# Start of a recurrence: whole first loads, key decay in one piece, another order on TensorE, three tiles for the rows of a batch

## The chip, the cores and the metric

The kernel runs on one core of a Trainium2 chip. Its engines each work through a list of their own and wait for each other with semaphores: TensorE (PE, matrix products; PEld is its loading of weights), VectorE (DVE), ScalarE (ACT), GpSimd (POOL) and SyncE (SP, which here only issues transfers). Products land in PSUM, in banks of 512 numbers a partition (the tiles of lines 63 to 67); all other tiles are in SBUF. The metric is the device time of one execution in microseconds; lower is better.

## What is computed

First a linear recurrence (RWKV-5) over 4 batches, 8 heads, 768 steps, with 48 numbers per head; then a routed layer (top 1 of 8 experts, 384 to 1024 to 384) on the 3072 rows that come out:

```python
for t in range(S):
    kt, vt, rt = (k[:, :, t], v[:, :, t], r[:, :, t])
    cur = np.einsum('bhd,bhe->bhde', u[None] * kt, vt)
    y[:, :, t] = np.einsum('bhd,bhde->bhe', rt, state + cur)
    state = w[None, :, :, None] * state + np.einsum('bhd,bhe->bhde', kt, vt)
...
logits = x @ w_gate
expert_idx = np.argmax(logits, axis=1)
...
    h = np.maximum(xe @ w1[e], 0.0)
    ye = h @ w2[e]
    out[mask] = gate_w[mask, None] * ye
```

All is done in 32-bit floats. `w` (the decay, between 0.85 and 0.95 here) and `u` belong to a head and are the same for all batches.

## The kernel before, in words

The recurrence is cut into 16 *units*, each a batch and a pair of heads (4 pairs), and each unit into 6 chunks of 128 steps. Within a chunk the work is a masked product; between chunks a small state is carried. A unit goes through these steps, each a function named in the code:

- `load_rk`, `load_vk`: SP issues the transfers of r and k (channels on partitions, the two heads at partitions 0 to 47 and 64 to 111) and of v and k (steps on partitions). There are three tiles `rks` and four tiles `vks`, used in turn. The arrays in memory hold zeros in the padding rows 48 to 63.
- `scale` (VectorE): r and k times the powers of w within a chunk, into `RKs`. The powers `TT` come from `decays` (a ladder on VectorE, with squares of w from POOL).
- `pairs` (POOL, for unit 0 VectorE): r times k into `rps`. `p_own` (TensorE): its sum with u over the channels, into the bank `dsb`. `own_t` (VectorE) transposes that, and `diag` (ACT, 12 instructions) puts it on the diagonals of `Aw`.
- `p_scores` (TensorE): the products within chunks, into the banks X0, X1 and X23; `mask` (VectorE, three instructions a unit) puts their upper triangles into `Aw`.
- `keys` (POOL or VectorE): k times the decay to the end of its chunk, into `Kds`. The decay `T3` comes from `key_decay` (VectorE and a wrapped copy on POOL) and `p_key_decay` (two transposes on TensorE for each head pair, then a copy on ACT).
- `p_ds` (TensorE): what each chunk adds to the state, into `dsb`; `scan` (VectorE) runs the state over the chunks.
- `p_out` (TensorE): the output, from `Aw` and the states, into the banks `yps`; `out_t` (ACT) copies it; `p_tr` (TensorE) turns it to rows and makes the logits; `keep` (ACT) copies that into the tile `xbs` of the batch, of which there are two. `send` (POOL) sends a batch's rows to their experts' places in memory, some turns after the batch is done.

The order on each engine is that in which the code lists the instructions: nothing reorders them. After a start written out by hand (lines 728 to 762), a loop of turns (763 to 828) runs unit i together with the output of unit i - 1 and the rows of unit i - 2. A copy of one number to `turn` on POOL (lines 751, 775, 781, 835) makes POOL wait there for another engine's result. `p_fill` issues products of the identity that nothing reads. From line 832 on come the experts; that part is the same in both kernels but for one name.

Before the first turn, `p_own` and `p_out` need banks without old contents in the rows that they don't write: line 730 copies zeros there on ACT. Lines 107 and 108 clear the padding rows of `rks[1]` and `rks[2]` on VectorE, since `load_rk` brings only the 48 channels of each head for all units but the first, whose load is whole and in two halves.

`key_decay` and `p_key_decay` are called for head pair 0 first (lines 736 and 741) and for the other three later (750 and 758). `load_rk(i + 3)` stands at the head of turn i (line 766).

## Time and profile before

| | us |
|---|---|
| median of five runs | 369.79 |
| lowest and highest of the five | 369.02, 369.98 |
| the profiled execution | 368.42 |
| its span, first to last instruction | 366.2 |
| TensorE busy | 349.6 |
| VectorE, POOL, ACT busy | 265.3, 210.9, 144.9 |
| mean clock granted to TensorE | 0.983 |
| turn 1 begins (first product of `p_own(1)`) | 19.93 |
| turns 2 and 3 begin | 24.83 and 30.67 |
| the last unit's turn ends, experts begin | 112.88 |

The profiled execution is one execution, and its times are not the median's: all times within the span are its own. In the views, a row of the timeline has a start in us, a duration, the engine, the line, the operation, and what it writes and reads; neighbouring instructions of the same kind are merged with their number (x16), and brackets give idle time of the engine before it and what ended it. One `nc.tensor.matmul` of 32-bit floats shows as two matmul records, so a `p_fill(8)` is x16. The clock is a share of full speed.

### The profile page before, as it was taken

To read this page: it belongs to the slowest core of one execution; us is meant where nothing else is said; L and a number is where in the kernel's file an instruction comes from. 1 tells how busy PE (TensorE), PEld (TensorE's weight loads), DVE (VectorE), ACT (ScalarE), POOL (GpSimd) and SP (SyncE) were. 2 spreads that over 40 slices of the span, in tenths; PEclk is the share of its full clock that TensorE was granted. 3 is DMA by queue.
4 is the path that set the end of the run, shared out by engine and by line. 5 is a ranking of instruction groups with operands and counts; after the bars stand their busy time and mean duration, and the time that the engine had idled before them with its cause. 6 is when DMAs were issued, how large, how long until landed. Compare 5 with 4: busy or idle time off the path is not lost.

```text
span 366.2 us, 9907 instructions
## 1 busy us (share of the span) xinstructions
PE 349.6 (95%) x3733; PEld 331.3 (90%) x3733; DVE 265.3 (72%) x659; ACT 144.9 (40%) x416; POOL 210.9 (58%) x262
## 2 busy tenths in 40 slices
PE   5799999999999999999999999999999999999991
PEld 5588887877888999999999999999999999999891
DVE  7777887887873328693897995898688788865531
ACT  4568877877885410322323312221230321113210
POOL 4859898999975530562116407904922951999342
PEclk9599999999999999999999999999999999999998
DMA  7998998978746895978459327624742943313401
GB/s 157 260 221 221 255 235 212 247 229 210 254 115 220 266 367 99 212 222 267 123 180 218 106 56 216 177 88 139 196 151 92 204 145 130 108 52 86 147 18 52
DMA packets 35610, 63.67 MB, mean 174 GB/s; under 512 B 18922, under 2 KB 20410, under 8 KB 35553
## 3 DMA queue, kind: packets, MB, share of 16 engines
q1 hardware_dynamic: 30048, 48.39, 50.3%
q0 software_dynamic: 3776, 9.84, 7.6%
q10 hardware_dynamic: 1728, 4.72, 3.8%
q8 instruction: 31, 0.51, 0.6%
q14 instruction: 27, 0.21, 0.2%
HBM read 51.82 MB, written 11.40 MB: 173 GB/s over the span
## 4 chain that ended last, share of the span: by engine, by line
PE 79%; ACT 6%; DVE 5%; issue 4%; POOL 3%; POOLq 0%; DVEq 0%; ACTq 0%
PE X L525 12%; PE X L587 10%; PE yps L629 9%; PE X L503 8%; PE tr L629 8%; PE yps L525 5%; ACT A L331 5%; PE dsb L629 4%; PE tr L525 3%; PE dsb L525 3%; PE yps L364 3%; PE yps L587 2%; PE X L325 2%; PE tr L382 2%; PE yps L369 2%
## 5 line engine op out<-in xcount | busy, mean ns | idle before, releaser
L702 POOL DMA_INDIRECT out_dram<-yo,ix x28 | 28.4, 1014 | 68.1 <-DVE so L647 43.1
L331 ACT ACTIVATE A<-eyes,own 128x128 f32<-128x128 f32 x192 | 58.0, 391 | 11.6 <-DVE own L315 10.1
L337 DVE COPY_PREDICATED A<-strict,X 128x512 f32<-128x512 int32 x48 | 34.7, 737 | 9.2 <-ACT xb L388 4.6
L587 PE MATMUL X<-hT,w2s 128*128 128x160 f32 (+5 forms) x288 | 36.5, 287 | 0.0
L587 PEld LDWEIGHTS X<-hT,w2s 128*128 128x128 f32 x288 | 36.2, 191 | 0.2
L436 POOL DMA_INDIRECT rows<-xb,slot x24 | 28.1, 1171 | 12.6 <-issue 5.1
L629 PE MATMUL yps<-tums,sums 128*128 128x192 f32 x184 | 32.3, 326 | 0.0
L629 PEld LDWEIGHTS yps<-tums,sums 128*128 128x128 f32 x184 | 30.3, 190 | 0.0
L702 POOL DMA_INDIRECT out_dram<-yt,it x16 | 16.8, 1048 | 20.5 <-DVE yt L654 9.4
L289 DVE TENSOR_TENSOR RK<-rk,TT 112x1536 f32<-112x1536 f32 (+1 forms) x17 | 27.7, 1636 | 0.0
L295 POOL TENSOR_TENSOR rp<-rk 112x768 f32<-112x768 f32 x15 | 27.3, 1817 | 0.0
L525 PE MATMUL X<-xT,w1s 128*128 128x208 f32 (+5 forms) x120 | 26.0, 331 | 0.0
L325 PEld LDWEIGHTS X<-RK 48*64 48x64 f32 x768 | 18.8, 137 | 7.6 <-issue 5.1
L716 POOL TENSOR_TENSOR tums<-w2s,tums 128x384 f32<-128x384 f32 x24 | 24.7, 1029 | 0.4
L364 PE MATMUL yps<-A,vk 128*48 128x128 f32 x384 | 24.0, 274 | 0.0
L325 PE MATMUL X<-RK 48*64 48x128 f32 (+1 forms) x768 | 21.9, 254 | 2.1 <-DVE RK L289 2.1
L525 PEld LDWEIGHTS X<-xT,w1s 128*128 128x128 f32 x120 | 20.9, 190 | 0.0
L364 PEld LDWEIGHTS yps<-A,vk 128*48 128x48 f32 x384 | 20.2, 123 | 0.4
L658 ACT ACTIVATE so<-so,xg 128x192 f32<-128x192 f32 x24 | 10.0, 450 | 25.2 <-DVE so L647 25.2
L663 ACT COPY so<-tr 128x192 f32<-128x192 f32 x7 | 2.2, 318 | 44.4 <-PE tr L629 44.4
L629 PE MATMUL tr<-w2s,hT 128*128 128x192 f32 x112 | 19.4, 326 | 0.0
L554 ACT ACTIVATE hT<-hT 128x416 f32<-128x416 f32 (+5 forms) x23 | 12.3, 537 | 17.6 <-DVE hT L546 17.6
(220 smaller groups left out, 842.9 us busy)
## 6 DMA issues: line engine op xcount, KB each, us to landing
w1s<-in_w_dram SPq DMA_DIRECT2D x36, 384.0 KB, 3.2
w2s<-in_w_dram SPq DMA_DIRECT2D x24, 384.0 KB, 3.4
rk<-in_rk_dram SPq DMA_DIRECT2D x30, 288.0 KB, 6.0
vk<-in_vk_dram SPq DMA_DIRECT2D x16, 528.0 KB, 5.5
w2s<-in_w_dram ACTq DMA_DIRECT2D x8, 384.0 KB, 5.9
xs<-rows SPq DMA_DIRECT2D x16, 169.0 KB, 5.6
w1s<-in_w_dram ACTq DMA_DIRECT2D x4, 384.0 KB, 3.3
rows<-zt SPq DMA_DIRECT2D x4, 312.0 KB, 4.8
```

Of the source, the lines that this page charges most:

```text
L289: nc.vector.tensor_tensor(RKs[i % 3][0:KP].rearrange("p u (c t) -> p u c t", t=C)[:, :, c0:c1], x[0:KP].rearrange("p u (c t) -> p u c t", ...
L295: (eng or nc.gpsimd).tensor_tensor(rps[i % 2][0:KP], x[0:KP, 0], x[0:KP, 1], op=ALU.mult)
L325: nc.tensor.matmul(o, lhsT=r[q, 1, c * C + 64 * z:c * C + 64 * z + 64], rhs=r[q, 0, c * C + 64 * z:(c + 1) * C], start=True, stop=True, sk ...
L331: nc.scalar.activation(A[:, place(c, h), :], eyes[:, c & 1, :], func=ACT.Copy, scale=own[i % 2][:, c, h:h + 1])
L337: nc.vector.copy_predicated(o, m, X01[k].rearrange("p (z c) t -> p z (c t)", z=2) if k < 2 else X23[:, :, 0:2 * C])
L364: nc.tensor.matmul(o(c, h), lhsT=v[:, c, h * D:(h + 1) * D], rhs=A[:, place(c, h), :], start=c < 2, stop=c == 0, skip_group_check=True)
L436: s_ = nc.gpsimd.indirect_dma_start(out=rows[:, :], out_offset=bass.IndirectOffsetOnAxis(ap=slot[b % 2][:, c:c + 1], axis=0), in_=xbs[b % ...
L503: nc.tensor.matmul(p[:, 0:self.n], lhsT=w1s[self.k % 2][f // 2][:, m, f % 2 * 128:(f % 2 + 1) * 128], rhs=self.t[:, m, 0:self.n], start=m ...
L525: nc.tensor.matmul(p[:, at * n:(at + 1) * n], lhsT=a, rhs=b, start=j == 0, stop=j == len(ab) - 1, skip_group_check=True)
L587: nc.tensor.matmul(p[:, 0:n], lhsT=w2s[self.k % 2][f // 2][:, f % 2, m * 128:(m + 1) * 128], rhs=self.h[:, f, self.c:self.n], start=f == 0 ...
L629: nc.tensor.matmul(p[:, at * Z:(at + 1) * Z], lhsT=a(f), rhs=b(f), start=f == 0, stop=f == FT // 2 - 1, skip_group_check=True)
L702: s_ = nc.gpsimd.indirect_dma_start(out=to[:, :], out_offset=bass.IndirectOffsetOnAxis(ap=at, axis=0), in_=x, in_offset=None, bounds_check ...
```

## The change

1. `xbs` has three tiles in place of two.
2. `load_rk` brings units 1 and 2 whole, padding included, in one transfer each (unit 0 whole in two halves as before, the others without padding in two transfers as before). The memsets of the padding go.
3. Zeros in the banks yps and dsb are written by VectorE's memset, at its very start, in place of ACT's copies; the tile `zero` goes.
4. `key_decay` is called once for all four head pairs. The transposes of pair 2 go to the first half and those of pair 3 to the second half of bank yps1 (before: yps0 and yps1).
5. The start on TensorE after `p_own(0)`: transposes of pair 0, the rest of `p_scores(0)`, transposes of pairs 1 to 3, `p_fill(6)`, `p_ds(0)`, `p_fill(3)`, `p_own(1)`. Before: transposes of pair 0, a third of `p_scores(0)`, `p_ds(0)`, the last third, transposes of pairs 1 to 3, `p_fill(8)`, `p_own(1)`.
6. On VectorE: `own_t(0)`, `scale(1)`, `keys(0)`, then two masks, `scan(0)` and the third mask. Before: the rest of `key_decay` behind `keys(0)`, then `scan(0)` and three masks. On POOL the order stays, with one wrapped copy in place of two.
7. `load_rk(i + 4)` stands in the middle of turn i, behind `pairs(i + 1)`, in place of `load_rk(i + 3)` at its head; unit 4 stays at the head of turn 1. On SP the transfers of r and k thus come before that turn's `load_vk(i + 3)` and not behind it.

```diff
+    for y in yps:
+        nc.vector.memset(y, 0.0)
+    nc.vector.memset(dsb, 0.0)
...
     def load_rk(i):
         if i < U:
             b, hp = divmod(i, HP)
-            if not i:
-
-                for q in (slice(0, S // 2), slice(S // 2, S)):
-                    nc.sync.dma_start(rks[0][0:KP, :, q], rk[b, hp].rearrange("h p u s -> (h p) u s")[0:KP, :, q])
-            else:
-
-                for h in range(2):
-                    nc.sync.dma_start(rks[i % 3][64 * h:64 * h + D], rk[b, hp, h, 0:D])
+
+            for q in (slice(0, S // 2), slice(S // 2, S)) if not i else (slice(0, S),) if i < 3 else ():
+                nc.sync.dma_start(rks[i % 3][0:KP, :, q], rk[b, hp].rearrange("h p u s -> (h p) u s")[0:KP, :, q])
+
+            for h in range(2) if i > 2 else ():
+                nc.sync.dma_start(rks[i % 3][64 * h:64 * h + D], rk[b, hp, h, 0:D])
...
-    for i in range(1, 3):
-        nc.vector.memset(rks[i][32:64], 0.0)
...
-    zero = cp.tile([128, 1], FP32, name="zero")
-    nc.gpsimd.memset(zero, 0.0)
...
-            o = (tr[:, 0:256], tr[:, 256:512], yps[0][:, 0:256], yps[1][:, 0:256])[hp]
+            o = (tr[:, 0:256], tr[:, 256:512], yps[1][:, 0:256], yps[1][:, 256:512])[hp]
...
-    xbs = [ca.tile([128, G, HP, Q], FP32, name=f"xb{i}") for i in range(2)]
+    xbs = [ca.tile([128, G, HP, Q], FP32, name=f"xb{i}") for i in range(3)]
...
     selection()
-    for y in (dsb, *yps):
-        nc.scalar.copy(y, bc(zero, [128, 512]))
     decays(0, HP)
     scale(0, 0, G // 2)
     p_scores(0, range(2))
     scale(0, G // 2, G)
     pairs(0, nc.vector)
-    key_decay(0, 1)
+    key_decay(0, HP)
     state_decay()
     p_own(0)
     own_t(0)
-    scale(1)
     p_key_decay(0, 1)
     p_scores(0, range(2, 4))
...
+    diag(0)
+    p_scores(0, range(4, G))
+    p_key_decay(1, HP - 1)
+    load_rk(3)
+    scale(1)
     keys(0, nc.vector)
-    diag(0)
-    load_rk(3)
-    key_decay(1, HP - 1)
+    p_fill(6, yps[0][:, 384:512])
     nc.gpsimd.tensor_copy(turn, RKs[1][0:1, 0, 0:1])
     pairs(1)
+    keys(1)
     p_ds(0)
-    scan(0)
     mask(0, 0)
     mask(0, 1)
-    p_scores(0, range(4, G))
-    p_key_decay(1, HP - 1)
-    keys(1)
+    scan(0)
     mask(0, 2)
-    p_fill(8, yps[0][:, 384:512])
+    p_fill(3, yps[0][:, 384:512])
     load_vk(3)
     for i in range(1, U):
         b, k = divmod(i - 6, 4)
         rt = i >= 6 and k == 0 and b < B - 1
-        load_rk(i + 3)
+        if i == 1:
+            load_rk(4)
         p_own(i)
...
             pairs(i + 1)
+            load_rk(i + 4)
             keys(i + 1, nc.vector if i in (7, 8, 11, 12) else None)
```

Every `xbs[b % 2]` becomes `xbs[b % 3]`.

## The prediction

> **What bounds the kernel now.** I read the page first, then who waited for whom, then the timeline of the first 40 us and the same stretch cut into windows for the clock.

> ```profile
> PE 349.6 (95%) x3733; PEld 331.3 (90%) x3733; DVE 265.3 (72%) x659; ACT 144.9 (40%) x416; POOL 210.9 (58%) x262
> ...
> PEclk9599999999999999999999999999999999999998
> ```

> TensorE is busy nearly everywhere; only the second slice (9.2 to 18.3 us) is at half clock. The waits of TensorE over the whole span:

> ```profile
> PE X L325 <- DVE RK L289: 2.1, 1, 2.1
> PE dsb L311 <- POOL rp L295: 1.8, 3, 0.9
> PE X L121 <- POOL zero L116: 1.4, 1, 1.4
> PE dsb L311 <- issue: 1.2, 1, 1.2
> PE dsb L344 <- DVE Kd L300: 1.2, 1, 1.2
> PE dsb L311 <- DVE S L349: 0.5, 1, 0.5
> ```

> Of these all but the second are before 25 us, and none is on a transfer. From turn 2 on (24.83) a turn takes 5.84 us of TensorE, save where batches are sent off. So what the change does to the time is how far it moves the first products of turn 2, p_own(2). The timeline up to there:

> ```profile
> 2.81 1.34 DVE L108 MEMSET rk<- 32x1536 f32 x1 [0.27 <-issue]
> ...
> 4.18 0.17 DVE L148 TENSOR_SCALAR pw<-wug 112x4 f32<-112x4 f32 x1
> ...
> 4.43 2.11 POOL L167 TENSOR_TENSOR pw<-pw 112x4 f32<-112x4 f32 x7 [0.93 <-DVE pw L148]
> ...
> 10.13 0.82 PE L311 MATMUL dsb<-rp,wug 112*2 112x192 f32 x8 [1.22 <-issue]
> ...
> 11.77 3.61 ACT L331 ACTIVATE A<-eyes,own 128x128 f32<-128x128 f32 x12
> ...
> 16.93 3.07 PE L121 MATMUL yps<-ident 128*128 128x128 f32 x16
> ...
> 19.93 0.51 PE L311 MATMUL dsb<-rp,wug 112*2 112x192 f32 x8
> ...
> 20.51 0.38 DVE L315 STREAM_TRANSPOSE own<-dsb 128x192 f32<-128x192 f32 x1 [3.18 <-PE dsb L311]
> ...
> 24.83 0.51 PE L311 MATMUL dsb<-rp,wug 112*2 112x192 f32 x8 [0.50 <-DVE S L349]
> ```

> Two chains are to be seen. Early, VectorE's two memsets (1.20 to 4.15) hold back the powers of w, and with them everything up to the diagonals at 11.77. Later TensorE itself is the chain: it works from 13.53 to 24.3 with no gap over 0.1, eight filler products (16.93 to 20.0) stand right before p_own(1), and rp(1), which p_own(1) reads, had been ready since 17.15. From p_own(1) on, own_t(1), the diagonals, mask and scan(1) lead 4.9 us later to p_own(2). The windows give the clock (columns: stretch, its length, PE, PEld, DVE, ACT, POOL busy, clock, DMA share, GB/s):

> ```profile
> 8.60:8.90 0.30, 0.30 (x16) 0.17 (x8) 0.30 (x1) 0.00 (x0) 0.00 (x0) 0.92 1.20 161
> 8.90:12.30 3.40, 2.18 (x28) 1.16 (x26) 2.54 (x5) 0.74 (x3) 1.94 (x3) 0.50 1.04 243
> 12.30:15.70 3.40, 2.24 (x41) 1.93 (x38) 3.40 (x6) 3.09 (x11) 3.23 (x13) 0.50 0.97 188
> 15.70:19.00 3.30, 3.21 (x15) 2.86 (x15) 1.63 (x3) 0.95 (x3) 2.75 (x3) 0.50 1.08 326
> 19.00:19.20 0.20, 0.20 (x4) 0.20 (x3) 0.00 (x0) 0.00 (x0) 0.00 (x0) 0.78 1.43 246
> ```

> The clock falls at 8.85 and is back at 19.09, 10.24 us later. A stretch of 3.4 us that is 64 or 66% busy did not bring it back; one 97% busy did. A filler pass takes 0.24 us before that edge and 0.13 after.

> **The change, part by part.** First the early chain, where the gain is. The two memsets of r and k go (2 x 1.34), three memsets of 128x512 in PSUM come. No row shows one: a third of the 1536-wide memset is 0.45, ACT's copy into the same banks 0.58, VectorE's mask of 128x512 out of PSUM 0.74. So they end between 2.55 and 3.42; I take 0.55 each, the nearest being the same engine's memset and the same bank's write: 2.85. The weights wug are there by 3.13 (ACT reads them then). But the powers run on POOL, and POOL is busy with strict and eyes until 3.50, less about 0.05 for the dropped memset of zero. The powers can start at 3.45 instead of 4.43: 0.98 gained, 0.86 at the dear end. ACT's three copies of zero (1.7 us) go too; ACT was idle behind them till 11.56, so that is worth nothing.

> Key decay whole: one product of 512 columns for one of 128 (0.28). The other 112x512 product took 0.69, so 0.41 more on VectorE, inside the 0.85 us in which it waited for p_own(0). POOL's wrapped copy grows from 64 to 256 columns (0.24 and, for 192, 0.34): 0.40, and the second transpose of head pair 0 waits for it: 0.1 lost. The later 1.18 and 0.34 go. So p_own(0) comes at 9.15, the diagonals at 10.9 instead of 11.77, and end at 14.5 instead of 15.38: 0.87 earlier.

> Now TensorE's new order. After p_own(0) and the first transposes (to 10.6) come the other two thirds of scores(0) (0.92 each, to 12.4) and the transposes of head pairs 1 and 2 (0.63 and 0.47, to 13.5). Pairs 2 and 3 now share the bank yps1, and by the built order pair 3's transposes wait for ACT's copy of pair 2. That copy stands behind the twelve diagonals and the copy of pair 1: 14.5 plus two steps of 0.35 with their end, 15.1. **Here is a new wait** of 1.6 us on TensorE, and queued behind it are six fillers, p_ds(0), three fillers and p_own(1). At half clock: transposes 0.47 to 15.57; 12 passes at 0.24, 2.84, to 18.4; p_ds(0) 1.15, of which 0.7 is done by 19.09 and the rest takes 0.26 at the ratio of its rows (0.65 against 1.15): 19.35. Then six passes at 0.13 to 20.13, beside which scan(0) (0.65, starting 0.12 after p_ds) ends at 20.12. p_own(1), which waits for scan(0), starts at 20.2: **0.3 later than 19.93**. The 0.97 gained upstream is eaten: the fillers start 1.3 earlier, but one more of them (0.47) and p_ds(0) (1.15) now stand in the row. mask(0,2) runs from 20.1 to 20.8 and own_t(1), due 20.8, just fits behind it. From there the chain of 4.3 us to p_own(2) is unchanged.

> The edits with no price, each with its cover. Whole loads of units 1 and 2: 688,128 instead of 589,824 bytes, but one issue instead of two and no wait for a memset. scale(1) would like rk at 10.4. Bytes moved by 9.0 us before: 1.41 MB, as much as wug, unit 0 and the larger unit 1 need. If it is late, scale(1) may slip 5 us before the masks (needed by scan(0) at 19.4) or scores(1) at 20.6 feel it. scale(1) and keys(0) stay behind own_t(0) on VectorE. pairs(1) on POOL: dec's copy ran until VectorE's products ended and 0.68 more; now to about 13.5, pairs(1) to 15.8, keys(1) to 17.1, both before 20.2. Loads of r and k in mid-turn: SP now issues rk(i+4) after pairs(i+1) and only then vk(i+3). In turn 1 vk(4) goes out at about 25.8 instead of 23.55, is there 5.5 later (median landing of vk) at 31.3, and is read at 35.05. The tightest is vk(12): 73.37 becomes about 74.5, lands by 80, read at 83.50; only a landing of 9 us would cost. Since no wait of TensorE is on a load, nothing can be gained. Three tiles xb: ACT's copies L387 in turns 10 and 14 (79.86, 105.34) start without idle time behind the diagonals, so the wait for the sends that goes was hidden: zero. The waits of turns 7 to 12 (rp late on POOL behind sends and sums) keep their places.

> Sum: +0.3 on the profiled execution's 368.42, so 368.7. The median of the five runs is 369.79, 1.37 above the profiled one; carried over: **370.1**.

> [...] In the new order the stretch from 8.9 to 12.3 is some 92% busy, between the 66% that did not bring the clock back and the 97% that did. If it does, the clock is full from 12.3, and then comes the stall of about 2 us at 13 to 15.1. The row: before, TensorE idled 2.07 us (6.28 to 8.35) and the clock fell at 8.85; so it would fall again at 15.7, and p_own(1) comes at 19.9: no change. [...]

> **Rivals.** *The clock is kept* (faster): granted before 13.4 and not lost in the stall. The 5.86 us of half-clock work from 15.1 (0.45 + 2.84 + 1.15 + 1.42) then takes 0.55 of that, 3.2, and p_own(1) starts at 18.35: 1.6 gained, 368.2. For it: the 92% stretch. Against: the fall at 8.85 after as short a stall. *The clock comes late* (slower): the new stall at 13.5 to 15.1 makes a 3.4 us stretch with part of it as poor as the 64% ones, so the edge may fall behind p_own(1). All 5.86 at half clock: 20.95, and p_own(1) itself 0.82 instead of 0.51: 1.3 lost, 371.1. It decides from an edge at about 20.3, where p_own(1) passes 20.67. For it: before, work ran on from 13.53, now only from 15.1. *A load is late*: vk(12) or the whole rk(1) as above; a landing of 13.5, the longest of vk, would cost vk(12)'s reader 4.5: 374. Against: that landing was in the crowded start.

> **How the numbers follow.** Edge near where it was, +0.0 to +0.3: 0.42. Clock kept, or early enough to gain over 0.74: 0.24. Clock late: 0.31; late load 0.03. 0.2% is 0.74 us, about what a measurement of this kernel can tell from none. Faster 0.24, same 0.42, slower 0.34. The likeliest alone lies in 369.6 to 370.6; with both clock cases, whose ends are 368.2 to 371.2, 8 in 10 are within 368.4 to 371.2.

> **What would show it.** Powers of w on POOL at 3.45; diagonals at 10.9; an idle TensorE from about 13.5 to 15.1, released by ACT; fillers at 15.6; p_own(1) near 20.2 and p_own(2) near 25.1, then turns of 5.84. Wrong if TensorE does not idle there, if the clock is full at 15.6, or if p_own in turns 7, 8, 9, 11 and 12 waits otherwise than by 0.26, 0.87, 0.25, 0.20 and 0.70.

## The result, and the profile after

The changed kernel takes 373.06 us in the median (369.30 to 381.59, 39 executions), the kernel before beside it 369.83 (368.58 to 374.48, 65 executions); the ratio is 1.0044, with an interval of 1.0028 to 1.0059. The ratio leaves out slow executions, those over 1.5% above the fastest of the same kernel, and the medians do not. The spread itself changed: of all executions in this study, 22 of 59 of the changed kernel were more than 5 us over the kernel before's median on the same chip, 7 of 24 of its version without the moved loads, 0 of 24 of the moved loads alone, and 3 of 181 of the kernel before. The forecast was 370.1 (368.4 to 371.2), no change likeliest; by the ratio the kernel is some 1.6 us slower, by the medians 3.2.

The first profiled execution took 376.77 us (span 374.6), so it is one of these 22. The page's busy time and clock, then the timeline of the start:

```profile
PE 353.1 (94%) x3735; PEld 334.2 (89%) x3735; DVE 267.4 (71%) x659; ACT 143.4 (38%) x413; POOL 208.3 (56%) x260
...
PEclk9599999988999999999999999999999999999997
```

```profile
3.44 2.15 POOL L164 TENSOR_TENSOR pw<-pw 112x4 f32<-112x4 f32 x7
...
9.13 0.82 PE L308 MATMUL dsb<-rp,wug 112*2 112x192 f32 x8 [1.17 <-DVE rp L292]
...
10.89 3.61 ACT L328 ACTIVATE A<-eyes,own 128x128 f32<-128x128 f32 x12
...
14.97 0.63 PE L182 MATMUL yps<-ident,T3c 112*128 112x112 f32 x2 [1.91 <-ACT T L183]
...
15.40 2.79 PE L118 MATMUL yps<-ident 128*128 128x128 f32 x12
...
18.12 1.04 PE L341 MATMUL dsb<-vk,Kd 128*48 128x48 f32 x20
...
20.08 0.51 PE L308 MATMUL dsb<-rp,wug 112*2 112x192 f32 x8
...
24.77 0.49 PE L361 MATMUL yps<-A,vk 128*48 128x128 f32 x5 [1.35 <-issue]
...
26.02 0.51 PE L308 MATMUL dsb<-rp,wug 112*2 112x192 f32 x8
```

Up to 20.08 this is the start as forecast: powers at 3.44, diagonals at 10.89, the new wait of TensorE on ACT's copy (1.91), p_own(1) at 20.08 where the kernel before has 19.93. Then comes a row that nothing in the kernel before resembles: TensorE stands still for 1.35 us in the middle of p_out(0), between two products that need nothing new, and what ended the stall is "issue": no semaphore. p_own(2) comes at 26.02 (24.83 before). Further on, in turn 10, the same happens at the transposes p_tr(8). The releaser that the row names, a diagonal on ACT, has nothing to do with these products, and yT, which they read, had been there since 77.9:

```profile
80.60 2.04 PE L379 MATMUL tr<-sel,yT 112*128 112x104 f32 x8 [1.80 <-ACT A L328]
```

The clock's windows around it (stretch, length, busy time of PE, PEld, DVE, ACT, POOL, then granted clock, DMA share, GB/s):

```profile
77.20:80.60 3.40, 1.61 (x57) 1.14 (x56) 3.23 (x9) 2.57 (x9) 3.10 (x4) 1.00 1.02 302
80.60:84.00 3.40, 3.40 (x26) 3.21 (x28) 1.32 (x2) 2.50 (x8) 3.24 (x4) 0.50 0.99 252
84.00:87.40 3.40, 3.40 (x43) 2.95 (x39) 2.15 (x7) 0.33 (x1) 0.74 (x4) 0.50 0.57 152
87.40:90.80 3.40, 3.40 (x73) 2.81 (x72) 1.88 (x2) 2.26 (x7) 2.45 (x2) 1.00 0.63 191
```

In the stretch with the stall TensorE is busy for 1.61 of 3.40 us; the next two run at half clock, and turn 10 takes 11.13 us instead of 6.51. So this execution lost 1.35 and 4.6 us in the turns of two stalls without a wait, one of them with a drop of the clock behind it. Two smaller losses in it are plain waits: p_own(8) on POOL's rp(8), behind a send that sat idle for 2.38 us for a load, and p_own(13) (1.57).

```profile
61.56 1.18 POOL L433 DMA_INDIRECT rows<-xb,slot  x1 [2.38 <-DMA rk<-in_rk_dram]
...
64.74 0.51 PE L308 MATMUL dsb<-rp,wug 112*2 112x192 f32 x8 [2.33 <-POOL rp L292]
```

**What "issue" may be.** The page's list of DMA queues has a line of 31 packets and 0.51 MB of kind "instruction", so some 16,400 bytes each (16,384 in the packets). I counted TensorE's records (a product and its weight load each, twice for 32-bit data, and the few of its sequencer) from 0 at the start of the trace. The stalls of 1.35, 0.28 (at 53.34) and 1.80 us stand before records 449, 1729 and 2753. Each of these is 193 more than a multiple of 256, as it would be if a packet held 256 of these records, 64 bytes for each; all 7557 make 29.5 such packets. *Theory F*: TensorE had run out of instructions, since the next block had not landed. Against it *theory W*: a wait on data or on another engine that the profile does not name. And on which edit costs: *theory B*, the moved loads; *theory S*, the reordered start; *theory I*, only both together.

### The profile page after: what moved, and what is told of

The parts are those of the page before. It is cut to its first block, busy times and chain, and to the rows that moved or that the text cites. A ratio compares the mean times of both kernels' runs of the same rounds, so it can differ in the third digit from the quotient of the medians.

```text
span 374.6 us, 9895 instructions
## 1 busy us (share of the span) xinstructions
PE 353.1 (94%) x3735; PEld 334.2 (89%) x3735; DVE 267.4 (71%) x659; ACT 143.4 (38%) x413; POOL 208.3 (56%) x260
## 4 chain that ended last, share of the span: by engine, by line
PE 79%; ACT 5%; issue 4%; DVE 4%; DMA 3%; POOL 3%; POOLq 0%; DVEq 0%; ACTq 0%; SPq 0%
PE X L522 12%; PE X L584 9%; PE yps L626 8%; PE X L500 8%; PE tr L626 8%; PE yps L522 5%; ACT A L328 4%; PE dsb L626 3%; PE yps L361 3%; DMA rows<-zt 3%; PE tr L522 3%; PE dsb L522 3%; PE tr L379 2%; PE yps L584 2%; PE X L322 2%
## 5 line engine op out<-in xcount | busy, mean ns | idle before, releaser
L433 POOL DMA_INDIRECT rows<-xb,slot x24 | 28.9, 1205 | 16.3 <-issue 5.4
L286 DVE TENSOR_TENSOR RK<-rk,TT 112x1536 f32<-112x1536 f32 (+1 forms) x17 | 29.7, 1754 | 1.1 <-DMA rk<-in_rk_dram 1.1
L699 POOL DMA_INDIRECT out_dram<-yt,it x16 | 16.8, 1047 | 20.5 <-DVE yt L651 9.4
L361 PE MATMUL yps<-A,vk 128*48 128x128 f32 x384 | 25.5, 283 | 1.3 <-issue 1.3
L713 POOL TENSOR_TENSOR tums<-w2s,tums 128x384 f32<-128x384 f32 x24 | 24.7, 1030 | 0.4
L361 PEld LDWEIGHTS yps<-A,vk 128*48 128x48 f32 x384 | 21.3, 128 | 2.0 <-issue 1.6
L379 PE MATMUL tr<-sel,yT 112*128 112x104 f32 x128 | 19.4, 295 | 1.9 <-ACT A L328 1.8
L655 ACT ACTIVATE so<-so,xg 128x192 f32<-128x192 f32 x24 | 10.1, 450 | 25.4 <-DVE so L644 25.4
L379 PEld LDWEIGHTS tr<-sel,yT 112*128 112x128 f32 x128 | 16.6, 199 | 3.3 <-ACT A L328 1.9
L626 PE MATMUL tr<-w2s,hT 128*128 128x192 f32 x112 | 19.4, 326 | 0.0
## 6 DMA issues: line engine op xcount, KB each, us to landing
vk<-in_vk_dram SPq DMA_DIRECT2D x16, 528.0 KB, 10.5
```

What stands on the lines that cost most here:

```text
L286: nc.vector.tensor_tensor(RKs[i % 3][0:KP].rearrange("p u (c t) -> p u c t", t=C)[:, :, c0:c1], x[0:KP].rearrange("p u (c t) -> p u c t", ...
L361: nc.tensor.matmul(o(c, h), lhsT=v[:, c, h * D:(h + 1) * D], rhs=A[:, place(c, h), :], start=c < 2, stop=c == 0, skip_group_check=True)
L379: nc.tensor.matmul(trv[c // 4][:, c % 4, :], lhsT=yTs[i % 3][0:KP, c & 1, (c // 2) * C:(c // 2 + 1) * C], rhs=sel[:, c & 1, i % HP, :], st ...
L433: s_ = nc.gpsimd.indirect_dma_start(out=rows[:, :], out_offset=bass.IndirectOffsetOnAxis(ap=slot[b % 2][:, c:c + 1], axis=0), in_=xbs[b % ...
L626: nc.tensor.matmul(p[:, at * Z:(at + 1) * Z], lhsT=a(f), rhs=b(f), start=f == 0, stop=f == FT // 2 - 1, skip_group_check=True)
L699: s_ = nc.gpsimd.indirect_dma_start(out=to[:, :], out_offset=bass.IndirectOffsetOnAxis(ap=at, axis=0), in_=x, in_offset=None, bounds_check ...
```

## Experiments

### Each part alone

On one chip: the kernel before with edit 7 alone, the changed kernel without edit 7, and the kernel before with edit 1 alone.

```diff
 # loads_mid: kernel before
-        load_rk(i + 3)
+        if i == 1:
+            load_rk(4)
...
             pairs(i + 1)
+            load_rk(i + 4)
 # loads_old: changed kernel, the same lines the other way round
 # tiles3: kernel before
-    xbs = [... for i in range(2)]
+    xbs = [... for i in range(3)]
```

> This is the kernel before with one part of the change alone: the loads of r and k for turn i+4 are issued behind the pairs of turn i+1 (and the fourth unit's at the head of turn 1), where they were issued for turn i+3 at the head of turn i. The start, the two batch tiles and the memsets stay. Theory B (the moved loads): on SyncE's queue the loads of r and k now stand ahead of the load of v and k and of the batch's clear of the rows, three in one burst, so v and k land later (median about 8 to 10.5 us from issue where the kernel before has 5.5), the clears later still (about 11 us against 4.8), and in turns 7 to 12 the first send of a batch or the keys wait for them: slower by 1 to 3 us (370.8 to 372.8 where the kernel before gives 369.8), with waits of 1 us and more before the own products of turn 8 or in the block of turn 10. Theory P (the prediction: a load that comes earlier or later within its slack gains and costs nothing): the time of the kernel before within 0.2% (369.1 to 370.5). Theory S (the reordered start costs everything): also the time of the kernel before.

> This is the changed kernel with the loads of r and k put back to the head of the turn (for turn i+3); the three batch tiles and the whole reordered start stay. Theory B (the moved loads cost most of the loss): turns 7 to 12 have the waits of the kernel before again, and what stays is the start: own products of turn 1 at about 20.1 and of turn 2 at about 25 to 26 (the 1.35 us that TensorE stands still inside the first output products in the changed kernel may stay, since it may come from the order of TensorE's instructions): 369.9 to 371.3 where the kernel before gives 369.8. Theory S (the reordered start costs everything, because it moves TensorE's program against something that runs by its own clock): as the changed kernel, 371.5 to 373, with the long turns 7, 10 and 12 still there.

> This is the kernel before with three tiles in place of two for the rows of a batch, and nothing else. The prediction priced this at nothing: no row of the kernel before shows a wait of ScalarE's copy into the tile or of GpSimd's numbers on the sends of the batch before. Expected: the time of the kernel before within 0.2%, whatever the theory on the rest. A loss or a gain of over 0.2% would say that the place of the tiles, or the numbers' earlier write, has a price that the trace of before does not show.

| | median, us | ratio to the kernel before (interval) | turns 1 and 2 begin |
|---|---|---|---|
| kernel before, same chip | 369.69 | | |
| moved loads alone | 369.79 | 1.0004 (0.9981 to 1.0027) | 20.64, 25.87 |
| all but the moved loads | 370.29 | 1.0014 (0.9989 to 1.0039) | 20.17, 25.07 |
| three tiles alone | 369.53 | 0.9988 (0.9966 to 1.0010) | 20.14, 25.05 |

Theory B expected 1 to 3 us from the moved loads and falls: by themselves they show no cost, with v and k landing 6.3 us after issue (5.5 in the kernel before; 10.5 in the first profile of the whole). Theory S expected the long turns 7, 10 and 12 without them; they were not there (7.30, 6.52 and 6.65 us in its one profile), so it falls too in this form. But 2 of the 12 executions without the moved loads took 378 us, so the start is not free in all of them. Three tiles are worth nothing, as forecast. What is left is that the parts together do what neither does, or that the first profile's chip was at fault. The edits of the start (2 to 6) were not tried one by one.

### Moving the block boundaries

Two kernels put more records on TensorE ahead of the suspected places.

```diff
 # fetch_shift: changed kernel, each of the twelve fillers at the very start as two of 64 columns (48 records more)
     for k in range(12):
-        p_fill(1, X01[k // 4][:, k % 4, :] if k < 8 else ...)
+        o = X01[k // 4][:, k % 4, :] if k < 8 else ...
+        for z in range(2):
+            nc.tensor.matmul(o[:, 64 * z:64 * z + 64], lhsT=ident, rhs=ident[:, 64 * z:64 * z + 64], ...)
 # tiny_shift: changed kernel, ahead of pair 3's transposes, where TensorE waits anyway (40 records more)
+            if hp == 3:
+                for _ in range(10):
+                    nc.tensor.matmul(yps[0][0:2, 384:392], lhsT=ident[:, 0:2], rhs=ident[:, 0:8], ...)
```

> This is the changed kernel with each of the twelve filler products at the very start split into two of 64 columns each: the same columns in sum, but 48 more instruction records on TensorE ahead of everything else. Theory F: the places where TensorE of the changed kernel stands still with no wait of its own (1.35 us inside the first output products, 1.80 us at the transposes of turn 7) are block boundaries of its instructions, all three found at places that are 193 more than a multiple of 256 instructions, where the next 16,384 bytes of instructions had not landed. Then these stalls leave the places where they were: the one of the first output products goes, because the boundary is now crossed at about 12 us instead of 16.7, so the own products of turn 2 start at about 24.9 instead of 26.0, and any stall left stands again at 193 more than a multiple of 256, some dozen products earlier in the program. Time: 0.8 to 4 us below the changed kernel's of the same chip. Theory W (the stalls are waits on data or on another engine): the stalls stay at the same products of the first output block and of turn 7's transposes, and the time is the changed kernel's within 0.3%.

> This is the changed kernel with ten products of 2 rows and 8 columns each put ahead of pair 3's transposes, where TensorE stands idle from 13.06 to 14.97 us anyway: 40 more instruction records on TensorE and, unlike the halved fillers, no time (about 1 us inside the idle). Theory F (instructions that land late): the boundary of instructions that is crossed at 16.7 in the changed kernel is crossed at about 13.3, its next block lands by 21, and the 1.35 us stall inside the first output products is gone: own products of turn 2 at 24.7 to 25.0 after those of turn 1 at 20.1; stalls left stand at places that are 193 more than a multiple of 256. Time 0.5 to 3 us below the changed kernel's. Theory B (the moved loads alone, through late v and k and late clears): turns 7 to 12 as long as in the changed kernel, time within 0.3% of it.

Both times theory F was right on the places; on the time it was wrong once and undecided once. With the halved fillers: 372.61 us, 1.0084 (1.0049 to 1.0118), in a set of runs without the changed kernel. They were not free: twice as many weight loads took 10.31 us instead of 4.67, p_own(0) came at 12.72 instead of 9.13, and that is the loss. But turn 1 took 4.91 us with no stall in it. The stalls were now before records 1473, 1729, 2497 and 2753, all again 193 more than a multiple of 256, but at other products. With the tiny products (0.65 us, inside the idle stretch), 377.73 us, 1.0016 (0.9982 to 1.0049) on a slower chip where the kernel before took 376.69. That is below the 1.0034 of the changed kernel there, as expected, but by less than the intervals can tell. In its profiled execution (383.36 us) turn 1 took 4.92, and a stall came one block later, before record 705. That is now a state product of unit 2, no longer an output product:

```profile
28.58 0.56 PE L345 MATMUL dsb<-vk,Kd 128*48 128x48 f32 x14
32.09 0.48 PE L345 MATMUL dsb<-vk,Kd 128*48 128x48 f32 x6 [2.95 <-issue]
32.30 2.84 PE L365 MATMUL yps<-A,vk 128*48 128x128 f32 x24
```

In the middle of one run of equal products, with all operands there, TensorE waits 2.95 us. Theory W falls: the stall stays at the count and not at the product. Over all profiles of this study, every stall of TensorE between 20 and 60 us that is longer than 0.25 us and has no wait of its own stands before such a record. In the packets of kind instruction, the block in question had landed shortly before each time:

| kernel | record | stall, us | block landed | TensorE went on |
|---|---|---|---|---|
| changed, first profile | 449 | 1.35 | 23.16 | 24.77 |
| changed, first profile | 2753 | 1.80 | 79.29 | 80.60 |
| halved fillers | 1729 | 1.35 | 54.52 | 56.32 |
| tiny products | 705 | 2.95 | 30.64 | 32.09 |
| first try (below) | 449 | 3.35 | 22.79 | 24.41 |
| third try (below) | 705 | 2.91 | 28.31 | 29.88 |

In the 27 such stalls of over 0.15 us, between 20 and 84 us, TensorE went on 1.20 to 1.80 us after the landing. Over the whole of all 17 profiles it enters 476 blocks, and not one sooner than 1.20 us after its landing. That is what theory F needs and what chance would not give. Most entries cost nothing of the kind: between 20 and 84 us it enters 171 blocks, and 144 of them without such a stall.

### The whole and its parts side by side

The changed kernel was run twice more, on two chips, and on the second of them together with both parts and one profile of the kernel before.

> This is the changed kernel itself once more, on the chip of the next two. Each part of the change alone left the time where it was (moved loads 1.0004 of the kernel before, the rest 1.0014), while the whole came to 1.0044 with a profiled execution of 376.8 us. Theory I (the two parts together lose what neither loses alone): median again 371 to 374, executions spread over 8 us and more, landings of v and k near 10 us, and in most profiles a stall of TensorE of over 1 us without a wait of its own. Theory C (the chip of the first measurement was to blame, whose packets took some 10% longer): median 370 to 371, landings of v and k at 5 to 7 us, no turn over 7.5 us.

> The changed kernel beside its parts on one chip. Theory I (the parts together lose what neither loses alone, because the reordered start brings TensorE to its second block boundary 1.8 us later, with less time to spare, while the moved loads keep more outstanding and so let blocks of instructions start later): 1.003 to 1.006 of the kernel before, above both parts by 0.002 and more; the parts at 0.999 to 1.0025. Theory A (the losses just add): the whole equals the sum of the two parts within 0.002. Theory C (it was chips): the whole at 0.999 to 1.002 here.

> The moved loads alone once more, beside the whole: 0.999 to 1.0025 of the kernel before by theory I; half of the whole's loss or more by theory A, if it is the loads that cost.

> The whole change without the moved loads, beside the whole: 1.000 to 1.0025 of the kernel before by theory I; half of the whole's loss or more by theory A, if it is the start that costs.

> The kernel before once more, for its profile on this chip: own products of turn 1 at 19.9 to 20.2, of turn 2 at 24.8 to 25.2, blocks of instructions that start 0 to 4 us after their crossings, and no stall of over 0.5 us without a wait before 60 us. If stalls of 1 us and more stand in it too, then late blocks alone do not set the changed kernel apart on this chip.

| | ratio to the kernel before (interval) | kernel before, median |
|---|---|---|
| whole, chip of the tiny products (again) | 1.0034 (1.0000 to 1.0068) | 376.69 |
| whole, another chip (again2) | 1.0100 (1.0035 to 1.0166) | 376.92 |
| moved loads alone, that chip | 0.9990 (0.9953 to 1.0027) | 376.92 |
| all but the moved loads, that chip | 1.0015 (0.9972 to 1.0058) | 376.92 |

Theory C (the chip) falls: the whole is slower in all three measurements, though the second interval reaches 1. Theory A (losses just add) would have 1.0005 for the whole on the last chip; the whole's interval excludes that, but the sum of the parts is itself known to only some 0.006, and the whole's six executions gave more than the 1.003 to 1.006 that theory I expected. The medians there are 381.71 us for the whole, 380.05 for all but the moved loads and 376.61 for the moved loads: in its long executions the start loses by itself. So that only the two together cost is not shown. What the stalls do is clearer from the profiles. First TensorE's waits from 5 to 60 us in the changed kernel (the last of its three profiles), then in the kernel before on the same chip (line and operand, releaser, sum, number, longest):

```profile
PE yps L182 <- ACT T L183: 2.7, 1, 2.7
PE yps L361 <- issue: 2.1, 4, 0.7
PE X L322 <- DVE RK L286: 1.5, 1, 1.5
PE dsb L308 <- DVE rp L292: 1.2, 1, 1.2
PE dsb L308 <- POOL Kd L297: 0.3, 1, 0.3
```

```profile
PE dsb L344 <- DVE Kd L300: 1.8, 1, 1.8
PE X L325 <- DVE RK L289: 1.4, 1, 1.4
PE dsb L311 <- issue: 1.2, 1, 1.2
PE dsb L311 <- DVE S L349: 0.5, 1, 0.5
PE dsb L311 <- POOL Kd L300: 0.3, 1, 0.3
```

The line with four waits for "issue" in the output products is the whole's alone; the moved loads alone and the rest alone have no such line on this chip. (The whole's second profile has three such stalls, 0.54, 0.54 and 0.96, before records 449, 705 and 961; all but the moved loads had two on its first chip, 0.18 and 0.50, and the moved loads alone one, 0.36 before record 2753.) Added up from 20 to 84 us, the stalls are 3.4, 2.0 and 2.1 us in the whole's three profiles, 0.7 and 0 without the moved loads, 0.4 and 0 with them alone, and 0 in the two of the kernel before and the one with three tiles. That is of the size of the loss. (The 1.2 for "issue" in the kernel before is the wait of p_own(0) at 10.1.) The timeline of the changed kernel shows the four:

```profile
19.67 0.51 PE L308 MATMUL dsb<-rp,wug 112*2 112x192 f32 x8
...
23.45 0.49 PE L361 MATMUL yps<-A,vk 128*48 128x128 f32 x5 [0.44 <-issue]
...
24.70 0.51 PE L308 MATMUL dsb<-rp,wug 112*2 112x192 f32 x8
...
29.71 0.81 PE L361 MATMUL yps<-A,vk 128*48 128x128 f32 x10 [0.36 <-issue]
...
31.29 0.51 PE L308 MATMUL dsb<-rp,wug 112*2 112x192 f32 x8
...
36.28 1.08 PE L361 MATMUL yps<-A,vk 128*48 128x128 f32 x15 [0.68 <-issue]
...
38.12 0.51 PE L308 MATMUL dsb<-rp,wug 112*2 112x192 f32 x8
...
42.68 1.30 PE L361 MATMUL yps<-A,vk 128*48 128x128 f32 x20 [0.57 <-issue]
```

The block boundary can be read without counting: the break in the output products leaves 5, 10, 15, then 20 records of them, because a turn has a few records more than a block and the boundary falls earlier in each. Turns 1 to 4 take 5.03, 6.58, 6.83 and 6.62 us, those of the kernel before on this chip 4.92, 5.84, 5.84 and 5.84. (Turn 2 is 0.74 longer with a stall of 0.36 in its rows: the two parts of the broken row take 1.05 and 0.81, where the whole row of 24 takes 1.48 in the kernel before.) The changed kernel starts turn 1 at 19.67 against 20.89, and turn 5 at 44.74 against 43.34: 1.2 us ahead becomes 1.4 behind in four blocks. It stays 0.7 to 1.4 behind to the last unit's turn, and the profiled executions differ by 1.68 us (378.12 against 376.44). The last 1.0 of the spans' difference of 1.8 comes after the start of turn 15, and I have not traced it.

One profile shows a drop of the clock without a late block. In the run of all but the moved loads on this chip, and in the kernel before, the windows with the wait of p_own(8) are these, one after the other:

```profile
61.90:65.30 3.40, 2.08 (x60) 1.49 (x57) 2.00 (x3) 2.12 (x7) 2.93 (x3) 1.00 0.89 200
65.30:68.70 3.40, 3.40 (x30) 3.21 (x30) 2.15 (x5) 3.05 (x10) 3.40 (x3) 0.50 0.80 251
```

```profile
61.70:65.10 3.40, 2.13 (x65) 1.50 (x58) 2.01 (x3) 1.76 (x6) 2.93 (x3) 1.00 0.91 257
65.10:68.50 3.40, 3.36 (x59) 3.18 (x60) 3.24 (x7) 3.34 (x12) 3.40 (x3) 1.00 0.84 244
```

Busy for 2.08 us (61%) the clock fell (turn 8 then took 9.75 us), busy for 2.13 (63%) it did not. Why the new start has more long executions, and whether they are such drops, is open.

### More bytes on their way

What makes a block late? A *crossing* is TensorE's first record of a block. Over nine traces, before 60 us, I set the time from a crossing to the start of the next block's packet against the bytes of loads under way at the crossing. With hardly any (under 70 KB) it was -0.7 to 0.3 us (so too in the second profile of the kernel before: crossing at 24.07, start at 24.19); with 300 KB and more mostly 1 to 6.5 us, and a line through the points (some 67, correlation 0.7) had a slope of about 2 us for 1000 KB. The test adds bytes to the kernel before:

```diff
     load_vk(3)
+    weights1(0)
```

> This is the kernel before with four loads of 384 KB more in SyncE's queue, behind the load of v and k of unit 3, issued at about 11.5 to 13.5 us: the first weights of one expert, loaded in their place long before they are wanted (they are loaded again later, as before). No instruction of TensorE, VectorE, ScalarE or GpSimd reads them there, so no wait on data is added to turns 0 and 1. Theory F (TensorE's instructions come as blocks of 16,384 bytes over the same DMA engines as the loads, and a block starts the later the more is on its way: over nine traces 1.2 us plus 1.9 us for each 1000 KB outstanding when TensorE crosses into the block before): the block that starts 3.5 us after the crossing at 14.9 in the kernel before starts 5 to 7 us after it, so 20 to 22, and TensorE stands still with no wait of its own for 0.5 to 3 us at its place 449 (193 more than 256), inside the first output products at about 23 us. Later, near 31 to 36 us, r and k of unit 4 may be waited for too, which is a plain wait on data. Theory W (the stalls have nothing to do with the loads on their way): no stall at 23 us, the block starts 3 to 4 us after the crossing as before, and only the wait near 31 to 36 us is there, if any.

Measured: 0.9983 (0.9953 to 1.0014). With 1536 KB more issued the block started 3.15 us after the crossing at 14.9, where the kernel before has 3.47 and 5.20 in its two profiles (neither of this set), and no stall came before record 449. One of 0.85 came before 961, two blocks on, with a start 4.11 us after its crossing. So the slope is no law, and theory F's number for it falls here. In the whole's last profile even the engines had room. From TensorE's crossing at 23.45 to the block's start at 26.96, the DMA engines' own line (busy tenths, slices of 0.09 us) and the packets of that stretch are

```profile
DMA  5555290526001101001008990306994938999900
...
q1 hardware_dynamic: 116, 0.52, 64.9%
```

and the block's packet comes first in the next 0.3 us:

```profile
q8 instruction: 1, 0.02, 25.7%
```

From 24.3 to 25.3 the engines were nearly idle, and the block had still not been started. So it was asked for later than the crossing, or held elsewhere. What exactly asks, and when, stays open, and with it why one stall is often followed by others in the next blocks.

### Tries at a faster version

The first try keeps the new start and the old place of the loads, uses TensorE's idle stretch for four of six fillers, and loads v and k of unit 1 sooner. The second also holds the load of v and k of unit 2 until pairs(1) is done; the third has 14 tiny products ahead of p_own(0) instead.

```diff
 # first try, against the changed kernel without edit 7
+    load_vk(1)
     load_rk(2)
-    load_vk(1)
...
         for hp in range(h0, h0 + nh):
+            if hp == 3:
+                p_fill(4, yps[0][:, 384:512])
...
-    p_fill(6, yps[0][:, 384:512])
+    p_fill(2, yps[0][:, 384:512])
 # second try, against the first
-    load_vk(2)
...
-    load_rk(3)
...
     pairs(1)
+    nc.gpsimd.memset(vks[2][0:1, 0, 0:1], 0.0)
+    load_vk(2)
+    load_rk(3)
     keys(1)
```

> A try at a version below both kernels: the changed kernel with the loads of r and k back at the head of the turn, four of the six fillers put ahead of pair 3's transposes (into TensorE's idle stretch from 13.06 to 14.97) and two behind them, and the first loads ordered so that v and k of unit 1 come before r and k of unit 2. Expected, if the start is bound by what TensorE does and by v and k of unit 1 (which landed at 19.65): TensorE's clock comes back at about 15.7 and not at 19.1, the state products of unit 0 start at 16.4 to 16.8 and not at 18.1, the own products of turn 1 at 17.8 to 18.6 and not at 20.1, those of turn 2 at about 23.4 (then r times k of unit 2 is what they wait for) and not at 25.1: 368.0 to 369.0 where the kernel before gives 369.7. If it is bound by what lands, as the kernel's DMA engines (99 of 100 busy from 3 to 40 us) would have it: the turns from the second on get the time back in waits, and the time is the one of the kernel before within 0.2%.

> This is the try of before once more (loads of r and k at the head of the turn, four fillers into the idle stretch, v and k of unit 1 ahead of r and k of unit 2), since it ran on a chip where the kernel before itself took 376.7 us and where blocks of instructions started late: own products of turn 1 came at 17.7 as expected, and then TensorE stood still for 3.35 us at its place 449, the block having started 6.4 us after its crossing. Expected on a chip of the first kind (kernel before near 369.7), by theory F: the block starts 4 to 5 us after the crossing at 15, lands by 20.5, and the stall is 0 to 1.5 us; own products of turn 2 at 22.5 to 24, and 367.5 to 369.5 for the whole, 0.9950 to 0.9995 of the kernel before. On a chip of the second kind: as before, 1.0047 of the kernel before.

> The same try with one thing more: the load of v and k of unit 2 is held until r times k of unit 1 is made (about 16 us), and the load of r and k of unit 3 follows it, so that at TensorE's crossing at 15 us some 500 KB less are outstanding and 576 KB less are issued while the block waits. By theory F the block starts 1 to 2.5 us sooner after the crossing than in the try without the hold, and TensorE's stall at place 449 is shorter by as much, or gone: own products of turn 2 at 22.4 to 23.2, 0.9935 to 0.998 of the kernel before on this chip. Against it: v and k of unit 2 land at 20 to 22, in time for GpSimd at 22.4, and r and k of unit 3 at about 24 to 25, against a need at about 24.5, so up to 0.5 us may come back as a wait there. By theory W the stall is as long as without the hold.

> The first try with, in place of the hold, fourteen products of 2 rows and 8 columns ahead of unit 0's own products, where TensorE waits 1.17 us for r times k anyway: 56 more instruction records, so that the crossing comes at about 11.5 and not at 15. By theory F the block starts at 15.5 to 18 and not at 19 to 21, and place 449 (now 56 records earlier in the program, in the scores or the state products of turn 1 at about 19.5) is reached with its instructions there: stall 0 to 1 us; own products of turn 2 at 22.4 to 23.4; 0.9935 to 0.999 of the kernel before. The next crossing is earlier by the same 56 records, so a stall may come back one block on. By theory W nothing changes against the first try.

| try | ratio (interval) | turn 1, turn 2 begin | stalls without a wait |
|---|---|---|---|
| first | 1.0047 (1.0003 to 1.0092) | 17.72, 25.66 | 3.35 before 449 |
| first, another chip | 1.0062 (1.0030 to 1.0094) | 18.82, 24.57 | 2.14 before 705 |
| second, that chip | 0.9984 (0.9956 to 1.0011) | 18.81, 24.27 | 0.29, 1.51, 0.30, 1.03 before 705, 961, 1217, 1729 |
| third, that chip | 1.0005 (0.9967 to 1.0042) | 18.56, 23.47 | 2.91 before 705 |

```profile
17.72 0.51 PE L310 MATMUL dsb<-rp,wug 112*2 112x192 f32 x8
19.80 1.26 PE L363 MATMUL yps<-A,vk 128*48 128x128 f32 x19
24.41 0.49 PE L363 MATMUL yps<-A,vk 128*48 128x128 f32 x5 [3.35 <-issue]
25.66 0.51 PE L310 MATMUL dsb<-rp,wug 112*2 112x192 f32 x8
```

The first try did on TensorE what was expected: the clock came back at 15.8, p_own(1) stood at 17.72 and rp(2), the next thing needed, was ready at 22.40. Then TensorE ran dry for 3.35 us, more than it had gained, and behind that stretch the clock stood at half from 26.05 to 32.88 and turn 2 took 8.94 us. The same with the tiny products: half clock from 30.80 to 44.46, turns 2 and 3 of 11.05 and 9.46. So a long stall cost more through the clock than by itself there: these two turns are 8.8 us longer than two of 5.84, of which the stall is 2.95. Holding a load worked at the place it was meant for: the block for record 449 started 1.15 us after its crossing, against 5.63 in the first try on that chip. Of the tests on loads this is the one that moved a block the way theory F expects. The stalls came in later blocks instead, each smaller than the first try's 2.14 there but 3.13 in sum, and p_own(2) at 24.27 missed the expected 22.4 to 23.2. None of these beats the kernel before beyond its interval. The start's gain is there to be had on the engines, and late blocks take it back.

## Why the prediction was wrong

- **The start was right**, step by step: powers 3.44 (3.45 forecast), p_own(0) 9.13 (9.15), diagonals 10.89 (10.9), TensorE idle before pair 3's transposes to 14.97 (15.1), fillers 15.40 (15.57), p_own(1) 20.08 (20.2). The memsets into PSUM measured 0.5 each (0.55 taken). The clock came back at 19.15, where the kernel before has 19.09, so the step on the clock held, and neither of its rivals came about. The stretch forecast as 92% busy was 94% (3.19 of 3.41 us) and did not bring the clock back. That the edge came within 0.1 us was in part luck: in the changed kernel's other two profiles it came at 18.87 and 18.30. By the ratio the measured time lies near the rival with the late clock (371.1), but not by its mechanism.
- **The step that failed is "From there the chain of 4.3 us to p_own(2) is unchanged"**, and with it "then turns of 5.84". The chain of data was unchanged. What broke it is not in that chain: 1.35 us without instructions in the first profile (p_own(2) at 26.02 instead of 25.1). In the other two p_own(2) came at 25.14 and 24.70, but then turns of 6.76 and 7.11, and of 6.58, 6.83 and 6.62, each with a stall without a wait. The sum put TensorE's own instruction stream at nothing, without a word; it cost 2.0 to 3.4 us of stalls a profile. The page's line of 31 instruction packets, and the fact that a turn of 5.84 us, with its 266 records, uses up a block of 256 in about 5.6, were there to be read.
- **The edits at no price**: three tiles (0.9988) and the moved loads by themselves (1.0004 and 0.9990) were priced rightly at nothing. "Since no wait of TensorE is on a load, nothing can be gained" was right. That nothing can be lost either was taken along, and may be wrong: on the last chip the whole has four stalls before 60 us where its parts have none, in one profile each. How much of that is the loads' is not shown, since the start without them has long executions too.
- **The landing carried over** from the kernel before, 5.5 us for v and k, was 10.5 in the first profile, and the rival of a late load in part happened there (p_own(8) waited 2.33). In the whole's last profile turns 6 to 8 have the lengths of the kernel before on that chip (6.59, 7.30, 6.63 against 6.59, 7.30, 6.62), so this is no steady part of the loss.
- **The row on the clock** (the fall at 8.85 behind 2.07 us without a product) was a good guide: later the clock fell behind windows of 3.4 us in which TensorE was busy for 1.61 us (changed kernel) and 2.08 (all but the moved loads), so idle for 1.79 and 1.32. Whether a full clock would have outlived the new stall was not shown: in the first profile it was at half from 8.91 to 19.15, all through it. The time of the first fall is not the same in all runs: it came anywhere from 7.75 to 11.5 us in the 16 profiles that have one at the start.

## What to carry to other kernels

Here TensorE is busy for 94% of the time with 3735 short products, and its instruction stream was a resource like any other: 266 records a turn against blocks of 256, and 2.0 to 3.4 us of stalls in each profile of the changed kernel. In a kernel like it, look for the queue of kind "instruction" on the page, count the records per turn against a block, and ask of a stall "issue" in the middle of equal instructions whether a block had not landed: each of the 27 here ended 1.20 to 1.80 us after a landing. A reordering that gains time on the engines of such a kernel, or moves loads to another moment, needs that margin checked, also where a part of it alone shows no loss in the ratio. A forecast of such an edit wants a range that reaches further on the slow side than the waits in the profile suggest.
